# First DFT of an AFNO block on one Trainium2 core: normalization factors folded into the DFT matrix, other queues for the last rows, another order of the lower weight parts

## Chip, cores and metric

The kernel runs on one core of a Trainium2 chip. The metric is the time of one execution on the device in microseconds (us). The engines are named as in the profile: PE (TensorE, matmul), DVE (VectorE), ACT (ScalarE), POOL (GpSimd) and SP (SyncE, which here only issues DMAs).

## What is computed

An adaLN block on 4096 rows of 640 values: layer norm of x with a scale and a shift from `c`, a spectral mixer (a 2-D real FFT over a 1 x 4096 grid, a two-layer block MLP per frequency, an inverse FFT), then layer norm and a SwiGLU feed-forward. The change touches only the start: layer norm, FFT and the weights of the two layers.

```python
    x = A_x
    mod = (_silu(c) @ w_mod).reshape(c.shape[0], 6, 1, -1)
    sa, ca, ga, sb, cb, gb = ...
    h = _layernorm(x, axis=-1) * (1 + ca) + sa
    x = x + ga * _A_ref(h, A_w1, A_b1, A_w2, A_b2)
    h = _layernorm(x, axis=-1) * (1 + cb) + sb
    x = x + gb * _B_ref(h, B_w_gate, B_w_up, B_w_down)

def _A_ref(x, w1, b1, w2, b2):
    Xf = rfft2(x, axes=(1, 2))              # H = 1, so one FFT of length 4096 per channel
    z = Xf.reshape(B, H, Wf, NB, BS)        # NB = 4 blocks of BS = 160 channels
    hr = zr @ w1[0] - zi @ w1[1] + b1[0];  hi = zi @ w1[0] + zr @ w1[1] + b1[1]
    hr, hi = relu(hr), relu(hi)
    or_, oi_ = (the same with w2, b2), then soft-shrink by 0.01
    return irfft2(or_ + 1j * oi_)
```

## The kernel before

**The FFT in two stages.** A row index is written as n = 32 n1 + n2. Stage A is a DFT over n1 (128 points): the partitions of a tile hold n1, so one matmul with the constant matrix `fa` (128 x 128) transforms one n2. Stage B is a DFT over n2 (32 points, matrix `tb`) for a chunk of frequencies; there are eight chunks (`NCH`). Behind stage B comes the first layer (`stage_l1`, with `w1a`, `w1b`, `w1c`), then the second (`stage_l2`, with `w2a`, `w2b`, `w2c` and the bias `b2t`), the soft-shrink and the first inverse stage.

**Stage A.** x is read as eight tiles `xa` of four n2 each: 128 partitions x 4 rows x 640. For each tile `ln_stats` (L401) takes mean and variance of each row on DVE, two statistics of 320 values per row, and forms `rs` (1/sqrt of the variance, by a power) and `nm` (minus mean times `rs`) on POOL. `ln_apply` (L411) normalizes every row over its 640 values, some rows on ACT and some on DVE. `dft_a` (L432) makes five matmuls of 512 columns: rows 0 to 3 with the first 128 channels of each of the four blocks, and a fifth with the remaining 32 channels of all rows and blocks. In fp32 each matmul is two passes on PE. `evac_a` (L442) copies the results back into `xa`. The loop runs `ln_stats(t + 2)`, `ln_apply(t + 1)`, `dft_a(t)`, `evac_a(t)`, `moves(t)`.

**From stage A to stage B.** The frequencies have to be brought together over all n2. Most go through four scratch tensors `s1` in DRAM (`write_s1`, then `load_g`). For chunk 0 the rows of the last two tiles go straight from SBUF to SBUF: `move_g` copies four pieces of each of tiles 6 and 7 into `g0`, two of the four on POOL's DMA queue and two on SP's.

**What sets the order.** Everything in this part is in program order on each engine (`manual_schedule`), so an instruction waits for its data and everything behind it on its engine waits too. The order on SP's queue is the order of the calls in `moves(t)`: a write that waits for ACT holds up the loads behind it.

**Weights in two parts.** The first and second layers multiply rounded values (fp32r) in a high and a low part. `weights_high` writes the high part (POOL for the first six of the twelve `w1` jobs, ACT for the other six), `weights_low` the lower part on DVE (value times sign, minus the high part, L286). Jobs 0 to 5 are for the first half of the outputs, 6 to 11 for the second; of six jobs three are 512 wide and three 128. The lower parts of `w2` are made by DVE (jobs `w2a`, `w2b`, `w2c`) and POOL (`weights_rest`).

**The scale 1 + ca and the second bias.** `first_scale` accumulates five products of `w_mod` and silu(c) on DVE into `acc0`, `remainders` copies its 32-channel ends into `wx0`, `columns` sums over the partitions on PE, and `ca1` is the result. `c` is loaded behind tile 6 of x. The second bias `b2` is loaded into one partition of `b2s`, spread to all partitions by three matmuls with ones (L481) and copied to `b2t` by ACT (L487). `idle(n)` is n matmuls whose result nobody reads.

**Stage B of chunk 0.** `stage_b` (L600) makes the DFT over n2 for blocks 0 and 4 (the remainders) and 1; `evac_b` writes `z` in a high part by ACT (L607) and a lower by DVE (L608), `evac_r` the same for the remainders `rz` (L630 on ACT, L640 on DVE).

Of the kernel before, what the change touches and what calls it, by code (L numbers as in the profile page):

```python
# [173 lines left out]
def body(tc, x, w1, b1, w2, b2, wg, wu, wd, c, wm, k_fa, k_tb, k_tx, k_bm, k_bx, k_ga, k_ge, k_id, out, dbg=None):  # L174
# [4 lines left out]
    def f32(ap):  # L179
        return ap.bitcast(F32)  # L180
# [21 lines left out]
    with ExitStack() as top:  # L202
# [35 lines left out]
        with ExitStack() as af:  # L238
# [50 lines left out]
            af.enter_context(tc.manual_schedule())  # L289
            nc.sync.dma_start(fa, k_fa)  # L290
# [45 lines left out]
            stx = ExitStack()  # L336
            xp = stx.enter_context(tc.tile_pool(name="xp", bufs=1, side="right"))
            rp = af.enter_context(tc.tile_pool(name="rp", bufs=1))
            b2t = rp.tile([P, 2, NB, BS], F32, name="b2t")
            with tc.tile_pool(name="sp", bufs=1) as sp:  # L340
                xas = []
                xts = {t: xp.tile([P, 4, D], F32, name=f"xa{t}") for t in (1, 2, 3, 0, 4, 5, 6, 7)}

                def load_x(t):
                    xa = xts[t]
                    if t < 3:
                        for i in range(4):
                            nc.sync.dma_start(xa[:, i, :], xv[:, 4 * t + i, :])
                    else:
                        nc.sync.dma_start(xa, xv[:, 4 * t:4 * t + 4, :])  # L350
                    xas.append(xa)


                def write_s1(t, f):
                    nc.sync.dma_start(s1[f][4 * t:4 * t + 4].rearrange("n r d -> r n d"),
                                      xas[t][(slice(0, 64, 4), slice(64, P, 4), slice(2, P, 4), slice(1, P, 2))[f]])

                for t in range(6):
                    load_x(t)
                wm1 = sp.tile([P, 5, D], F32, name="wm1")  # L360
                stats = {}
                pas = {}
                raws = {}


                def moves(t):
                    if t < 6:
                        write_s1(t, 0)
                    if t < 4:
                        write_s1(t, 1)  # L370
                    if t == 0:
                        load_x(6)
                        nc.sync.dma_start(c5, c)
                    elif t == 1:
                        load_x(7)
                        raws[1] = load_weights(sp, w1, "1")
                    elif t == 2:
# [2161 lines left out]
```

## Time and profile before

| quantity | value |
|---|---|
| time, median of 3 runs | 1412.85 us (1411.89 to 1417.92) |
| profiled execution: time | 1411.32 us |
| profiled execution: span from the first to the last instruction | 1409.5 us |
| granted PE clock | 1.0 |
| busy over the span: PE, DVE, ACT, POOL | 98%, 76%, 54%, 43% |
| busy from 18 to 40 us (22 us): PE, DVE, ACT, POOL | 20.09, 21.60, 19.92, 10.55 us |
| busy from 50 to 56 us (6 us): PE, DVE, ACT, POOL | 4.58, 5.18, 4.81, 2.42 us |
| first matmul of stage A | 7.98 us |
| last matmul of stage A ends | 49.3 us |
| first matmul of stage B | 55.84 us |

Times in a timeline are microseconds from the start of the span. A row of the timeline gives start, length, engine, line, operation, what is written and read, a count where neighbours are merged, and in brackets how long the engine stood idle ahead of it and what ended that. "L286" is line 286 of the kernel. Lengths of neighbours can overlap, since an engine begins one instruction while the one before it drains.

### The profile page before, as it was taken

To read this page: it belongs to the slowest core of one execution; us is meant where nothing else is said; L and a number is where in the kernel's file an instruction comes from. 1 tells how busy PE (TensorE), PEld (TensorE's weight loads), DVE (VectorE), ACT (ScalarE), POOL (GpSimd) and SP (SyncE) were. 2 spreads that over 40 slices of the span, in tenths; PEclk is the share of its full clock that TensorE was granted. 3 is DMA by queue.
4 is the path that set the end of the run, shared out by engine and by line. 5 is a ranking of instruction groups with operands and counts; after the bars stand their busy time and mean duration, and the time that the engine had idled before them with its cause. 6 is when DMAs were issued, how large, how long until landed. Compare 5 with 4: busy or idle time off the path is not lost. (4 is left out here: it accounts for less than half of the span.)

```text
span 1409.5 us, 23754 instructions
## 1 busy us (share of the span) xinstructions
PE 1382.5 (98%) x8410; PEld 1310.7 (93%) x8410; DVE 1067.8 (76%) x1861; ACT 765.0 (54%) x1542; POOL 604.6 (43%) x683
## 2 busy tenths in 40 slices
PE   6899999999999999999999999999999999999998
PEld 2599999967999889899999999999999999999998
DVE  8889888889888888649787668678678757375644
ACT  6879999755555554436454345546164624262341
POOL 5700200157766594326445534447153624042241
PEclk9999999999999999999999999999999999999999
DMA  9876466675998897898877998696998668956634
GB/s 371 310 244 211 157 196 193 203 232 170 327 353 308 308 335 263 293 368 308 308 225 281 375 330 288 236 326 230 375 330 309 217 218 282 350 194 217 199 115 149
DMA packets 171016, 377.34 MB, mean 268 GB/s; under 512 B 22193, under 2 KB 81649, under 8 KB 168882
## 3 DMA queue, kind: packets, MB, share of 16 engines
q1 hardware_dynamic: 161794, 359.28, 73.6%
q0 software_dynamic: 6800, 13.93, 3.1%
q10 hardware_dynamic: 2304, 2.62, 0.5%
q8 instruction: 66, 1.08, 0.3%
q14 instruction: 52, 0.43, 0.1%
HBM read 269.48 MB, written 96.80 MB: 260 GB/s over the span
## 5 line engine op out<-in xcount | busy, mean ns | idle before, releaser
L1442 DVE TENSOR_TENSOR wb<-r,wb 128x768 fp32r<-128x768 f32 (+3 forms) x170 | 170.4, 1013 | 13.5 <-ACT wb L1435 13.3
L2050 PE MATMUL pw<-h,wt 128*128 128x384 f32 x412 | 139.3, 338 | 0.6 <-ACT s_y L2069 0.6
L2052 PE MATMUL pw<-h,wt 128*128 128x384 f32 x412 | 138.3, 336 | 0.0
L2051 PE MATMUL pw<-h,wt 128*128 128x384 f32 x412 | 138.1, 335 | 0.0
L1435 ACT ACTIVATE wb<-r 128x768 fp32r<-128x768 f32 (+3 forms) x168 | 104.5, 639 | 56.3 <-PE pw L2063 41.7
L2351 PE MATMUL pc<-wq,L 128*128 128x320 f32 x846 | 132.7, 309 | 0.9 <-DMA wq<-wqd 0.9
L2110 POOL TENSOR_TENSOR sg<-s_x,sg 128x384 f32<-128x384 f32 x24 | 30.0, 1250 | 234.5 <-DVE s_x L2076 234.5
L2351 PEld LDWEIGHTS pc<-wq,L 128*128 128x128 f32 x846 | 126.3, 188 | 1.1 <-DVE x L2308 1.1
L2130 DVE TENSOR_TENSOR L<-sg,L 128x384 fp32r<-128x384 f32 x144 | 101.0, 725 | 27.7 <-ACT L L2126 27.2
L2069 ACT ACTIVATE s_x<-pw 128x384 f32<-128x384 f32 x52 | 25.6, 492 | 164.2 <-PE pw L2052 162.3
L2050 PE MATMUL pw<-h,wb 128*128 128x384 f32 x312 | 105.0, 336 | 0.0
L2051 PE MATMUL pw<-h,wb 128*128 128x384 f32 x312 | 104.4, 335 | 0.0
L2052 PE MATMUL pw<-h,wb 128*128 128x384 f32 x312 | 104.4, 335 | 0.0
L2121 POOL TENSOR_TENSOR sg<-sg,sg 128x384 f32<-128x384 f32 x72 | 91.9, 1276 | 23.4 <-DVE L L2130 20.0
L1973 PE MATMUL pg<-ht,wb 128*128 128x512 f32 x260 | 101.8, 392 | 0.0
L2351 PE MATMUL pe<-wq,L 128*128 128x320 f32 x648 | 101.7, 309 | 0.0
L1974 PE MATMUL pg<-ht,wb 128*128 128x512 f32 x260 | 101.3, 390 | 0.0
L1975 PE MATMUL pg<-ht,wb 128*128 128x512 f32 x260 | 101.2, 389 | 0.0
L2267 PE MATMUL pd<-wq,a 128*128 128x320 f32 x632 | 96.8, 310 | 0.0
L2351 PEld LDWEIGHTS pe<-wq,L 128*128 128x128 f32 x648 | 96.6, 188 | 0.0
L2267 PEld LDWEIGHTS pd<-wq,a 128*128 128x128 f32 x632 | 93.5, 188 | 0.5
L772 POOL DMA_DIRECT2D s<-co x28 | 15.7, 559 | 175.9 <-ACT co L771 175.9
(317 smaller groups left out, 3914.1 us busy)
## 6 DMA issues: line engine op xcount, KB each, us to landing
wq<-wqd SPq DMA_DIRECT2D x83, 640.0 KB, 6.1
wt<-td SPq DMA_DIRECT2D x103, 512.0 KB, 5.4
hs<-ho SPq DMA_DIRECT2D x52, 512.0 KB, 5.2
h<-hs SPq DMA_DIRECT2D x32, 768.0 KB, 7.9
td<-wt SPq DMA_DIRECT2D x25, 512.0 KB, 6.3
r<-in_B_w_gate_dram SPq DMA_DIRECT2D x24, 384.0 KB, 4.4
r<-in_B_w_up_dram SPq DMA_DIRECT2D x24, 384.0 KB, 4.3
xx<-tt SPq DMA_DIRECT2D x56, 160.0 KB, 3.3
```

Of the source, the lines that this page charges most:

```text
L1435: def high(ks, e=slice(0, c), copy=lambda o, i: act.activation(o, i, AF.Copy)):
L1442: dve.tensor_tensor(wbs[t, n][:, 1, ks, e], raw[t, n][:, ks, e], f32(wbs[t, n][:, 0, ks, e]), op=OP.subtract)
L1973: mm(b, wh, hh, start=(kk == 0), stop=False)
L1974: mm(b, wh, hl, start=False, stop=False)
L1975: mm(b, wl, hh, start=False, stop=(kk == 4))
L2050: mm(b, w(0, kp), a[:, kp, 0], start=start and kp == 0, stop=False, skip_group_check=not start)
L2051: mm(b, w(0, kp), a[:, kp, 1], start=False, stop=False, skip_group_check=not start)
L2052: mm(b, w(1, kp), a[:, kp, 0], start=False, stop=kp == 1, skip_group_check=not start)
L2121: pool.tensor_tensor(o, x, y, op=op)
L2130: dve.tensor_tensor(o[:, 1], raws[j], f32(o[:, 0]), op=OP.subtract)
L2267: mm(b[:, :320], l, m, start=start and i == 0, stop=stop and i == len(s) - 1)
L2351: mm(o[:, :320], ls[q][:, x, k], w[:, q, y], start=start and q == 0 and n == 0, stop=q == 1 and n == 2, skip_group_check=not start)
```

## The change

**Normalization in the DFT matrix.** For tiles 1 to 6 the rows are no longer normalized over 512 of their 640 channels. `scaled` multiplies the DFT matrix `fa` by `rs` (a factor per partition, that is per n1) for each row, into `wts` (rows 0 to 2 on ACT, row 3 on POOL; for tile 1 all on ACT). The matmul of a row uses its own scaled matrix. The mean's part is a sixth product per tile: `fa` with the four columns `nm`; `bias_a` copies its result to `bts`, and the evacuation of rows 0 to 3 adds it as a bias per partition. The remaining 4 x 32 channels of a row are still normalized in place (`rest`: rows 0 and 1 on ACT, 2 and 3 on DVE). Tiles 0 and 7 keep whole normalized rows (`ln_row`: ACT for tile 0, DVE for tile 7).

**Order of stage A.** Statistics are formed in groups of two rows (tiles 2 to 7), one tile ahead of the DFT instead of two, and the evacuation of a tile stands behind the preparation of the next. All evacuations are on ACT but one, row 3 of tile 7.

**Queues.** Of the eight `move_g` copies only one, row 0 of tile 7, stays on POOL's queue; seven are on SP's. `c` is loaded first on ACT's queue, and silu(c) comes at once. `b2` is loaded into all partitions by one DMA behind the loads of chunk 1, instead of one partition, matmuls and copies. The first half of `w2` is loaded behind the writes of tile 5 and 1.

**Other edits.** Fourteen idle matmuls stand at the start and six, not four, ahead of stage B. Of the lower parts of `w1`, job 0 stands ahead of the last evacuation, 1 to 5 ahead of `ca1`, 6 ahead of the first `z`, and 7 to 11 behind the first `rz`. `stage_b`, `evac_b` and `evac_r` are moved up in the text and `rz` goes to another pool.

```diff
+            nc.scalar.dma_start(c5, c)
             nc.sync.dma_start(fa, k_fa)
...
+                act.activation(sc, c5, AF.Silu)
+                idle(14)
...
                     if t < 6:
                         write_s1(t, 0)
+                    else:
+                        for i in range(4):
+                            move_g(0, t, i, pool if t == 7 and i == 0 else nc.sync)
...
-                        nc.sync.dma_start(c5, c)
...
-                        nc.sync.dma_start(b2s[0:1], b2.rearrange("r b o -> (r b o)").unsqueeze(0))
                     elif t == 4:
                         load_g(0, (0, 1))
-                        raws[2] = load_weights(rp, w2, "2", (0,))
                     elif t == 5:
                         for f in (2, 3):
                             write_s1(1, f)
+                        raws[2] = load_weights(rp, w2, "2", (0,))
                     elif t == 6:
-                        for i in range(4):
-                            move_g(0, t, i, (pool, nc.sync)[i // 2])
                         load_g(0, (2,))
-                    elif t == 7:
-                        for i in range(4):
-                            move_g(0, t, i, (pool, nc.sync)[i // 2])
...
+                def ln_stats(t, rows=range(4)):
+                    n = 1 if t < 2 else 2
+                    for i in rows[::n]:
                         mv, rs = layer_stats(lp, xas[t][:, i:i + n, :], n, f"a{t}_{i}")
...
+                def ln_row(t, i):
...
+                def scaled(t, *rows):
...
+                    for i in rows:
+                        if t > 1 and i == 3:
+                            pool.tensor_scalar(wts[t][:, i, :], fa, stats[t, i][1], None, op0=OP.mult)
+                        else:
+                            act.activation(wts[t][:, i, :], fa, AF.Copy, scale=stats[t, i][1])
+
+                def rest(t, *rows):
+                    for i in rows:
                         mean, rs, nm = stats[t, i]
+                        v = xas[t][:, i, :].rearrange("p (b e) -> p b e", b=NB)[:, :, 128:160]
+                        if i < 2:
+                            act.activation(v, v, AF.Identity, bias=nm, scale=rs)
                         else:
+                            dve.tensor_scalar(v, v, mean, rs, op0=OP.subtract, op1=OP.mult)
...
                 def dft_a(t):
                     xnr = xas[t].rearrange("p a (b e) -> p a b e", b=NB)
+                    plain = t in (0, 7)
+                    for i in (4, 0, 1, 2, 3) if t == 7 else (0, 1, 2, 3, 4) if t == 0 else (0, 1, 2, 3, 5, 4):
+                        pa = pas[t, i] = bank_a(f"pa{t}_{i}")
+                        if i == 5:
+                            mm(pa[:, 0:4], fa, nms[t], start=True, stop=True)
+                        elif i == 4:
+                            mm(pa, fa, xnr[:, :, :, 128:160], start=True, stop=True)
+                        else:
+                            mm(pa, fa if plain else wts[t][:, i, :], xnr[:, i, :, 0:128], start=True, stop=True)
+
+                def bias_a(t):
+                    bts[t] = sp.tile([P, 4], F32, tag="bt", bufs=3, name=f"bt{t}")
+                    act.activation(bts[t], pas[t, 5][:, 0:4], AF.Copy)
...
+                        elif t in bts:
+                            act.activation(xa[:, i, 0:512], pas[t, i], AF.Identity, bias=bts[t][:, i:i + 1])
...
+                for t in range(2, 7):
+                    ln_stats(t + 1, A)
+                    rest(t, 2, 3)
+                    ln_stats(t + 1, B)
+                    if t < 6:
+                        scaled(t + 1, 3)
+                    scaled(t, 0, 1)
+                    bias_a(t - 1)
+                    rest(t, 0, 1)
+                    if t == 2:
+                        evac_a(1, 0, 1)
+                    scaled(t, 2)
+                    evac_a(t - 1, *((2, 3) if t == 2 else (0, 1, 2, 3)))
+                    evac_a(t - 1, 4)
                     dft_a(t)
+                    moves(t - 1)
+                prep1 = prep_weights(raws[1], w1a, w1b, w1c, True)
+                for job in prep1[:6]:
+                    weights_high(*job, pool)
+                for i in range(4):
+                    ln_row(7, i)
+                first_scale(0, 3)
+                bias_a(6)
+                evac_a(6, 0, 1, 2, 3, 4)
+                dft_a(7)
+                moves(6)
+                first_scale(3, 5)
+                remainders(acc0, wx0)
+                weights_low(*prep1[0])
+                evac_a(7, 0, 1, 2, 3, 4)
+                moves(7)
 
                 pm1 = columns(acc0, wx0)
...
+                idle(6)
                 for job in prep1[6:]:
                     weights_high(*job)
...
+                for job in prep1[1:6]:
                     weights_low(*job)
+                dve.tensor_scalar(ca1, pm1[:, 0:5], 1.0, None, op0=OP.add)
...
+                load_tb(1)
+                nc.sync.dma_start(b2t.rearrange("p r b o -> p (r b o)"),
+                                  b2.rearrange("r b o -> (r b o)").unsqueeze(0).to_broadcast([P, 2 * NB * BS]))
...
+                for n in (1, 0):
+                    weights_high(*prep2[n])
+                weights_low(*prep1[6])
+                evac_b(0, 0)
+                evac_r(0, 0)
+                for job in prep1[7:]:
+                    weights_low(*job)
```

The order of instructions, as the built programs have it. First ACT, one tile in the middle of stage A. Before: the normalization of tile 5's first rows (`xa_120`), then the five evacuations of tile 4 (`xa_119`), then two rows of tile 6.

```order
L418 ACTIVATE xa_120<-xa_120,nm_0_384,rs_a_0_381 128x640 x3
L450 ACTIVATE xa_119<-pa_0_437 128x512
L450 ACTIVATE xa_119<-pa_1_439 128x512
L450 ACTIVATE xa_119<-pa_2_441 128x512
L450 ACTIVATE xa_119<-pa_3_443 128x512
L448 ACTIVATE xa_119<-pa_4_445 128x4x128
L418 ACTIVATE xa_121<-xa_121,nm_0_430,rs_a_0_427 128x640 x2
```

Now: two scaled matrices of tile 4 (`wt_395`), the bias of tile 3 (`bt_457`), remainders of two rows of tile 4 (`xa_120`), the third matrix, then the evacuations of tile 3 (`xa_118`).

```order
L491 ACTIVATE wt_395<-fa,rs_a_0_374 128x128 x2
L531 ACTIVATE bt_457<-pa_5_417 128x4
L498 ACTIVATE xa_120<-xa_120,nm_377,rs_a_0_374 128x4x32 x2
L491 ACTIVATE wt_395<-fa,rs_a_2_390 128x128
L541 ACTIVATE xa_118<-pa_0_409,bt_457 128x512
L541 ACTIVATE xa_118<-pa_1_411,bt_457 128x512
L541 ACTIVATE xa_118<-pa_2_413,bt_457 128x512
L541 ACTIVATE xa_118<-pa_3_415,bt_457 128x512
L537 ACTIVATE xa_118<-pa_4_419 128x4x128
```

The row products of 640 are gone, and six short instructions per tile stand in their place.

Then POOL, from the last square roots of tile 7 to the copy into `g0`. Before:

```order
L197 TENSOR_SCALAR rs_a_0_473<-mv_a_0_460 128x4
L198 TENSOR_TENSOR rs_a_0_473<-rs_a_0_473,mhalf 128x4
L406 TENSOR_TENSOR nm_0_476<-mv_a_0_460,rs_a_0_473 128x4
L407 TENSOR_TENSOR nm_0_476<-nm_0_476,mone 128x4
L281 TENSOR_SCALAR w1a<-rm_320 128x4x128
L281 TENSOR_SCALAR w1b<-rm_320 128x4x128
L281 TENSOR_SCALAR w1c<-rr_321,sgn 128x4x128
L281 TENSOR_SCALAR w1a<-rm_320 128x4x32
L281 TENSOR_SCALAR w1b<-rm_320 128x4x32
L281 TENSOR_SCALAR w1c<-rr_321,sgn 128x4x32
L316 DMA g_453<-xa_121 4x4x640 x2
L316 DMA g_453<-xa_122 4x4x640 x2
```

Now, from the scaled matrix of tile 6 (`wt_514`) on:

```order
L489 TENSOR_SCALAR wt_514<-fa,rs_a_2_509 128x128
L197 TENSOR_SCALAR rs_a_0_552<-mv_a_0_545 128x2
L198 TENSOR_TENSOR rs_a_0_552<-rs_a_0_552,mhalf 128x2
L197 TENSOR_SCALAR rs_a_2_565<-mv_a_2_558 128x2
L198 TENSOR_TENSOR rs_a_2_565<-rs_a_2_565,mhalf 128x2
L281 TENSOR_SCALAR w1a<-rm_362 128x4x128
L281 TENSOR_SCALAR w1b<-rm_362 128x4x128
L281 TENSOR_SCALAR w1c<-rr_363,sgn 128x4x128
L281 TENSOR_SCALAR w1a<-rm_362 128x4x32
L281 TENSOR_SCALAR w1b<-rm_362 128x4x32
L281 TENSOR_SCALAR w1c<-rr_363,sgn 128x4x32
L317 DMA g_541<-xa_123 4x4x640
```

Statistics are worked on in two halves, the means of tile 7 are not formed, and one copy stands behind the six products where four stood.

Last DVE, around the first `z` of stage B. Before, all lower parts of `w1` stand ahead of it:

```order
L286 SCALAR_TENSOR_TENSOR w1a<-rm_320,w1a 128x4x128
L286 SCALAR_TENSOR_TENSOR w1b<-rm_320,w1b 128x4x128
L286 SCALAR_TENSOR_TENSOR w1c<-rr_321,w1c 128x4x128
L286 SCALAR_TENSOR_TENSOR w1a<-rm_320,w1a 128x4x32
L286 SCALAR_TENSOR_TENSOR w1b<-rm_320,w1b 128x4x32
L286 SCALAR_TENSOR_TENSOR w1c<-rr_321,w1c 128x4x32
L608 SCALAR_TENSOR_TENSOR z_0_663<-pb_0_646,ca_68,z_0_663 128x2x256
L640 SCALAR_TENSOR_TENSOR rz_666<-pb_4_651,ca_68,rz_666 32x256 x2
L608 SCALAR_TENSOR_TENSOR z_1_671<-pb_1_656,ca_68,z_1_671 128x2x256
```

Now:

```order
L286 SCALAR_TENSOR_TENSOR w1a<-rm_362,w1a 128x4x128
L359 SCALAR_TENSOR_TENSOR z_0_734<-pb_0_716,ca_68,z_0_734 128x2x256
L391 SCALAR_TENSOR_TENSOR rz_737<-pb_4_721,ca_68,rz_737 32x256 x2
L286 SCALAR_TENSOR_TENSOR w1b<-rm_362,w1b 128x4x128
L286 SCALAR_TENSOR_TENSOR w1c<-rr_363,w1c 128x4x128
L286 SCALAR_TENSOR_TENSOR w1a<-rm_362,w1a 128x4x32
L286 SCALAR_TENSOR_TENSOR w1b<-rm_362,w1b 128x4x32
L286 SCALAR_TENSOR_TENSOR w1c<-rr_363,w1c 128x4x32
L359 SCALAR_TENSOR_TENSOR z_1_751<-pb_1_726,ca_68,z_1_751 128x2x256
```

Five of the six lower parts of the second half moved from ahead of the first `z` to behind the first `rz`.

427 lines of the change are left out of this document (208 added, 219 removed).

## Prediction

> **What bounds the kernel now.** First the table of stretches, busy time of each engine in pieces of the span: one row of the loop over x, one from behind it.
>
> ```profile
> core 0: us, PE busy (x) PEld busy (x) DVE busy (x) ACT busy (x) POOL busy (x), PEclk, DMA share, GB/s
> 18.00:40.00 22.00, 20.09 (x46) 8.06 (x45) 21.60 (x69) 19.92 (x34) 10.55 (x21) 1.00 1.01 410
> 80.00:120.00 40.00, 40.00 (x318) 40.00 (x317) 34.05 (x68) 35.37 (x74) 1.13 (x2) 1.00 0.60 190
> ```
>
> From 80 us on PE is busy all the time, so what the change gains or loses in the first DFT reaches the end only as far as it moves the point from which PE no longer stops. The waits of PE between 56 and 72 us say where that point lies:
>
> ```profile
> PE pb L600 <- DMA g<-xa: 1.4, 1, 1.4
> ...
> PE pc L711 <- DVE w2c L286: 0.5, 1, 0.5
> ```
>
> Two things count: when the last rows of x land in `g0` (L600, stage B), and when DVE has finished the lower part of `w2c`. The timeline of DVE, with PE's start of stage B:
>
> ```profile
> 54.53 0.69 DVE L286 SCALAR_TENSOR_TENSOR w1b<-rm,w1b 128x512 fp32r<-128x512 f32 x1
> ...
> 56.14 0.28 DVE L286 SCALAR_TENSOR_TENSOR w1c<-rr,w1c 128x128 fp32r<-128x128 f32 x1
> 57.73 0.75 DVE L608 SCALAR_TENSOR_TENSOR z<-pb,ca,z 128x512 fp32r<-128x512 f32 x1 [1.31 <-ACT z L607]
> 58.87 0.97 DVE L640 SCALAR_TENSOR_TENSOR rz<-pb,ca,rz 32x256 fp32r<-32x256 f32 x2 [0.40 <-ACT rz L630]
> ...
> 60.85 0.98 DVE L640 SCALAR_TENSOR_TENSOR rz<-pb,ca,rz 32x256 fp32r<-32x256 f32 x2 [0.23 <-ACT rz L630]
> ...
> 65.98 1.69 DVE L286 SCALAR_TENSOR_TENSOR w2b<-rm,w2b 128x640 fp32r<-128x640 f32 x1
> ...
> 69.16 0.89 DVE L286 SCALAR_TENSOR_TENSOR w2c<-rr,sgn,w2c 128x640 fp32r<-128x640 f32 x1
> ...
> 55.84 2.92 PE L600 MATMUL pb<-tb,g 128*128 128x128 f32 x24 [1.43 <-DMA g<-xa]
> ```
>
> From the first `z` at 57.73 to the end of `w2c` at 70.05 DVE stands still only 0.40 + 0.23 us: this chain of 12.32 us, hung on stage B's start, sets PE's last stop, at 70.2. The five lower parts from 54.53 to 56.42 (1.89 us) are free, since DVE then waits 1.31 us for stage B.
>
> What sets 55.84 is POOL, which copies four pieces of x into `g0` behind its six `w1` products. Its timeline, and the row of those copies among the DMAs (microseconds to landing last):
>
> ```profile
> 39.24 1.25 POOL L198 TENSOR_TENSOR rs_a<-rs_a,mhalf 128x4 f32<-128x4 f32 x1
> ...
> 41.28 1.75 POOL L281 TENSOR_SCALAR w1a<-rm 128x512 fp32r<-128x512 f32 x1
> ...
> 47.56 1.01 POOL L281 TENSOR_SCALAR w1c<-rr,sgn 128x128 fp32r<-128x128 f32 x1
> 48.53 1.40 POOL L316 DMA_DIRECT2D g<-xa  x2
> 50.23 1.13 POOL L316 DMA_DIRECT2D g<-xa  x2 [0.30 <-ACT xa L448]
> ...
> g<-xa POOLq DMA_DIRECT2D x4, 40.0 KB, 5.0
> ```
>
> Products from 41.28 to 48.57 (7.29 us), four copies, the last issued in the second half of 50.23 to 51.36, that is near 50.8, and 5.0 us to landing: 55.8.
>
> **The loop over x, engine by engine.** Three rows of the timeline (statistics and aggregates of one tile on DVE, the last four tiles on PE), then groups of the first 72 us by shape (busy, mean ns):
>
> ```profile
> 18.16 3.24 DVE L193 BATCH_NORM_STATS2 st_a<-xa 128x6 f32<-128x320 f32 x8
> 21.33 0.41 DVE L195 BATCH_NORM_AGGREGATE mv_a<-st_a 128x2 f32<-128x12 f32 x4
> ...
> 31.56 17.74 PE L439 MATMUL pa<-xa,fa 128*128 128x512 f32 x40 [1.81 <-ACT xa L418]
> ...
> 35.04 3.24 DVE L193 BATCH_NORM_STATS2 st_a<-xa 128x6 f32<-128x320 f32 x8
> ...
> L416 DVE TENSOR_SCALAR xa<-xa,mv_a,rs_a 128x640 f32<-128x640 f32 x13 | 7.4, 608 | 0.9 <-POOL rs_a L198 0.9
> L418 ACT ACTIVATE xa<-xa,nm,rs_a 128x640 f32<-128x640 f32 x19 | 16.9, 928 | 5.3 <-POOL nm L407 5.3
> L450 ACT ACTIVATE xa<-pa 128x512 f32<-128x512 f32 x28 | 14.6, 604 | 2.0 <-PE pa L439 1.9
> L607 ACT ACTIVATE z<-pb,ca 128x512 fp32r<-128x512 f32 x4 | 2.8, 689 | 1.9 <-PE pb L600 1.8
> L283 ACT ACTIVATE w1a<-rm 128x128 fp32r<-128x128 f32 x1 | 0.3, 298 | 0.0
> L198 POOL TENSOR_TENSOR rs_a<-rs_a,mhalf 128x4 f32<-128x4 f32 x6 | 7.1, 1177 | 0.5
> L198 POOL TENSOR_TENSOR rs_a<-rs_a,mhalf 128x1 f32<-128x1 f32 x8 | 4.5, 569 | 0.7
> L281 POOL TENSOR_SCALAR w1c<-rr,sgn 128x128 fp32r<-128x128 f32 x1 | 1.0, 1012 | 0.0
> L281 POOL TENSOR_SCALAR w1a<-rm 128x128 fp32r<-128x128 f32 x1 | 0.5, 523 | 0.0
> L430 DVE SCALAR_TENSOR_TENSOR acc<-wm,sc,acc 128x640 f32<-128x640 f32 x4 | 3.8, 952 | 0.1
> L446 DVE COPY xa<-pa 128x512 f32<-128x512 f32 x4 | 2.6, 683 | 0.5 <-PE pa L439 0.5
> ```
>
> *DVE* was full in this loop (21.60 of 22.00). A tile's eight statistics take 3.24 us, four aggregates 0.41; both stay. One to four row products of 608 ns go; two remainders of a fifth of the elements come, whose price lies between that fifth, 0.12, and the whole 0.61; I take 0.2 each, near the lower end. With the aggregates in two groups instead of one (up to 0.2 more) that is 4.05 to 4.25 us per tile. Now the statistics of tiles 3 and 7 begin 16.88 us apart, 4.22 per tile. DVE gains next to nothing: the statistics fill it, not the products.
>
> *ACT.* Out go two or three row products of 928 ns per tile. In come three scaled matrices (above 298, the same width without a factor per partition, and below 689, four times as wide with one; 390 taken), a copy of four columns (below 298; 200 taken), two remainders (298 to 928; 450 taken), and a bias in four evacuations: 689, the same width with one such operand, for 604. With the fifth evacuation as now that is 5.6 us, less some 0.09 for each of eleven neighbours that overlap: 4.6 to 4.7 us per tile. The second table load leaves the stream.
>
> *PE.* A tile's ten passes take 17.74 / 4 = 4.4 us, and a small product of four columns joins them (below one product more, 0.9; 0.1 taken): 4.5.
>
> *POOL.* Per half tile the power is 0.77 (on the line from 569 at one column to 1177 at four), with three short ones and gaps 1.8 us; two halves and one scaled matrix of 0.52 to 1.01 us make 4.1 to 4.6 us. With one power of 1177 for a whole tile it was about 2.5.
>
> So four engines end between 4.05 and 4.7 us per tile, and the loop doesn't get shorter. Ahead of tile 3 DVE has the same statistics as now, so its start stays near 18; the last aggregates then come at 18.0 + 5 x 4.25 = 39.2. POOL, by then some 0.4 behind, needs 1.2 for the last square root and starts the products at 40.8, against 41.28.
>
> **The sum.** Products 40.8 + 7.29 = 48.1; one copy there, landing 5.0 later, and 0.3 to PE as now: stage B at **53.4**, 2.4 us earlier. The three copies on SyncE come late too: DVE normalizes its last two rows until 42.1, forms `acc0` (five of 952 ns) and `wx0` (0.3) until 47.2, one lower part until 47.8, then copies row 3 (683 ns) until 48.5. How long 40 KB take on that queue no row shows; the bounds are
>
> ```profile
> fa<-in_k_fa_dram SPq DMA_DIRECT2D x1, 64.0 KB, 1.9
> ...
> s<-xa SPq DMA_DIRECT2D x14, 160.0 KB, 6.7
> ```
>
> and so a landing between 51.0 (with 0.6 of issue) and 55.8; with 4 us, between the two since other transfers run, 53.1: beside POOL's. Then the new order gives back: five lower parts, 1.89 us, stand between `rz` and the second `z`, in the chain that has only 0.23 us of slack there: 1.7 us. POOL's `w2` products, beside which `w2b`'s lower part took 1.69 against 0.89 for `w2c`, are then about 1 us further on; that is worth 0 to 0.8, and I take 0.5. **Net gain 2.4 - 1.7 + 0.5 = 1.2 us.**
>
> Costed at nothing, with what hides it: the idle passes at the start (PE waits for the first row); the sums of the second bias and their copies, which go (PE and ACT wait for 55.84 there; without that cover they would be worth 2.4 us); four moves of tile 6 on SyncE, which waits for ACT then; and `w2`'s first half, now loaded behind three writes: its reader on ACT comes just ahead of stage B's first `z`, so that a late load would hold up `z`, and DVE behind it, by as much. The bias, now 640 KB behind `tb` of chunk 1:
>
> ```profile
> 65.69 0.57 SPq L298 DMA_DIRECT2D tb<-in_k_tb_dram  x1
> ...
> 73.38 0.89 DVE L713 TENSOR_TENSOR tt<-pc,b2t 128x320 f32<-128x320 f32 x2
> ```
>
> Issued 0.6 behind `tb`, 2.4 earlier than now, and landing within 6.7 us it is there at 70.6; DVE wants it at 72.2. If it is late, `h` and `u` behind it on DVE wait, and PE for them.
>
> The profiled execution took 1411.32 us (span 1409.5), 1.5 less than the median of the runs shown, 1412.85. Less 1.2 these are 1410.1 and 1411.6; I take **1411.0**.
>
> **Rivals.**
>
> *DVE is the bound.* If SyncE's small copies land in 2 us and POOL's products run in half their time, DVE runs through: copy until 48.5, five lower parts and `ca1` 2.5, a sixth 0.6, then the chain, 12.3 + 1.7: 65.6 against 70.05, 4.5 us less: 1407.5. For it: the order of the lower parts would then cost nothing. Against it: the 7.29 us of the six products are in the trace, and they start behind the same statistics. 0.22.
>
> *POOL holds the loop back, and the new order costs.* Two rows show POOL's spread at one shape and operation; the first ran beside DVE's lower parts:
>
> ```profile
> L528 POOL TENSOR_TENSOR w2a<-rm,w2a 128x640 fp32r<-128x640 f32 x1 | 3.1, 3114 | 3.4 <-ACT w2a L283 3.4
> L528 POOL TENSOR_TENSOR w2b<-rm,w2b 128x640 fp32r<-128x640 f32 x1 | 1.5, 1542 | 0.1
> ```
>
> If a tile takes POOL 5.1 us instead of 4.6, five tiles put its products 2.5 us later, at 43.3, stage B at 55.9, and the lower parts then cost their 1.7 us: 1413.3. The sign turns where the products start at about 42.0. For it: POOL's work per tile nearly doubles, in short instructions beside a full DVE. Against it: beside the same statistics the power takes its 1177 ns now. 0.17. [...]
>
> **Chances.** Forecast 0.54 (1409.5 to 1412.5), DVE bound 0.22, POOL 0.17, the rest 0.07: a late `w2`, bias or load of x, or a gain beyond DVE's. The range, 1406.0 to 1415.0, takes in the first three and the spread of the runs shown. 0.5% is about 7 us, what a measurement of this kernel can tell from no change; no case reaches it but the tails: faster 0.04, same 0.94, slower 0.02.
>
> **What would show it.** POOL's first `w1` product at 40.8 (42.0 or later: the rival); stage B at 53.4, released by a copy into `g0`; five lower parts between `rz` and the second `z`, `w2c` done near 68.9, and PE without a stop from there. The forecast is wrong if stage B comes before 50, or if DVE waits for the bias, the statistics for x, or ACT for `w2`.

## Result and the profile after

| | kernel before | changed kernel |
|---|---|---|
| time, median | 1412.37 us (4 runs, 1410.84 to 1417.92) | 1420.30 us (4 runs, 1419.37 to 1422.65) |
| profiled execution: time, span | 1411.32, 1409.5 us | 1419.37, 1417.6 us |
| granted PE clock over the span | 1.000 | 0.994 |

The ratio is 1.0058, 95% interval 1.0038 to 1.0078: slower by about 8 us, where 1.2 us less had been forecast. Timed again beside the kernel before (e6 below), it was 1420.42 against 1413.65 us, ratio 1.0040 (1.0024 to 1.0056).

The loop over x itself went as planned. These are the stretches of the changed kernel, the same columns as before, with the two in which stage B starts, then the kernel before around its stage B:

```profile
core 0: us, PE busy (x) PEld busy (x) DVE busy (x) ACT busy (x) POOL busy (x), PEclk, DMA share, GB/s
18.00:40.00 22.00, 22.00 (x58) 10.08 (x58) 21.64 (x73) 21.73 (x53) 16.98 (x45) 1.00 1.01 418
50.00:60.00 10.00, 5.53 (x26) 5.56 (x27) 2.50 (x7) 2.47 (x6) 8.88 (x5) 0.68 0.92 324
60.00:70.00 10.00, 8.60 (x64) 7.83 (x63) 9.78 (x18) 8.51 (x19) 3.40 (x5) 0.98 0.91 300
80.00:120.00 40.00, 40.00 (x317) 40.00 (x316) 33.90 (x68) 34.99 (x72) 1.12 (x2) 1.00 0.54 183
```

```profile
50.00:56.00 6.00, 4.58 (x25) 3.41 (x26) 5.18 (x13) 4.81 (x11) 2.42 (x3) 1.00 0.78 203
56.00:70.00 14.00, 11.32 (x89) 10.47 (x88) 11.83 (x20) 11.63 (x24) 12.10 (x9) 1.00 0.95 360
```

From 18 to 40 us PE, DVE and ACT are all full. From 50 to 60 us DVE and ACT work a quarter of the time and PE about half of it, and the column PEclk reads 0.68, where the kernel before has 1.00. The timeline says what PE and SyncE did there, and POOL's first product and copy:

```profile
40.29 1.51 POOL L281 TENSOR_SCALAR w1a<-rm 128x512 fp32r<-128x512 f32 x1
47.01 1.05 PE L328 MATMUL pmc<-ones,acc 128*128 128x1 f32 x8 [0.24 <-DVE acc L509]
48.23 0.79 POOL L317 DMA_DIRECT2D g<-xa  x1
48.14 1.82 SPq L317 DMA_DIRECT2D g<-xa  x3
48.14 1.58 PE L335 MATMUL pz<-ones 128*128 128x128 f32 x12
54.47 5.46 PE L351 MATMUL pb<-tb,g 128*128 128x128 f32 x24 [4.74 <-DMA rr<-in_A_w_dram]
57.28 0.75 DVE L359 SCALAR_TENSOR_TENSOR z<-pb,ca,z 128x512 fp32r<-128x512 f32 x1 [6.27 <-ACT z L358]
60.24 0.69 DVE L286 SCALAR_TENSOR_TENSOR w1b<-rm,w1b 128x512 fp32r<-128x512 f32 x1
60.84 2.05 DVE L286 SCALAR_TENSOR_TENSOR w1c<-rr,w1c 128x512 fp32r<-128x512 f32 x1
70.10 0.88 DVE L286 SCALAR_TENSOR_TENSOR w2c<-rr,sgn,w2c 128x640 fp32r<-128x640 f32 x1
```

Before, PE did this ahead of stage B:

```profile
49.99 1.05 PE L327 MATMUL pmc<-ones,acc 128*128 128x1 f32 x8 [0.69 <-ACT xa L448]
51.13 2.40 PE L481 MATMUL pb<-b2s,ones 128*128 128x512 f32 x6
53.36 1.05 PE L334 MATMUL pz<-ones 128*128 128x128 f32 x8
```

Stage B starts at 54.47 instead of 55.84, but its 24 passes take 5.46 us instead of 2.92, after PE stood still for 4.74 us instead of 1.43. (The releaser named is a load of `w2`, which stage B does not read.) Of the eight copies into `g0`, the trace has a landing for the one on POOL's queue alone:

```profile
g<-xa POOLq DMA_DIRECT2D x1, 40.0 KB, 5.1
```

It was issued at 48.23 and so had landed at 53.3, 1.1 us before PE started. What was still to land then was on SyncE's queue.

The lower part of `w2c` starts at 70.10 instead of 69.16. Fine stretches of the same kernel give the clock around this place and around two later ones:

```profile
53.50:54.25 0.75, 0.00 (x0) 0.00 (x0) 0.00 (x0) 0.00 (x0) 0.75 (x2) 0.58 0.88 290
54.25:55.00 0.75, 0.53 (x2) 0.56 (x3) 0.00 (x0) 0.00 (x0) 0.75 (x1) 0.50 1.01 406
59.50:60.25 0.75, 0.75 (x6) 0.75 (x5) 0.70 (x3) 0.28 (x1) 0.67 (x2) 0.50 0.85 294
60.25:61.00 0.75, 0.75 (x7) 0.75 (x7) 0.75 (x2) 0.72 (x2) 0.75 (x1) 0.87 1.27 352
326.50:327.00 0.50, 0.50 (x3) 0.50 (x4) 0.50 (x2) 0.00 (x0) 0.00 (x0) 0.69 1.10 442
329.50:330.00 0.50, 0.50 (x3) 0.41 (x2) 0.30 (x1) 0.00 (x0) 0.00 (x0) 0.50 1.07 383
514.67:515.33 0.66, 0.66 (x4) 0.66 (x4) 0.49 (x1) 0.06 (x1) 0.00 (x0) 0.50 0.76 131
516.67:517.33 0.66, 0.66 (x4) 0.66 (x3) 0.66 (x2) 0.05 (x1) 0.00 (x0) 0.50 1.09 377
```

Summed over all stretches, the clock is at half for 6.8 us from 53.6 us on, for 3.4 us from 326.7 and for 3.4 us from 514.4, and for no time in the profile of before. (A last stretch, at the end of the span, lies behind the last matmul and is left out here and below.) PE's waits, the longest of after, then the same two products in before (`py` is a product of the last inverse stage, `gt` its matrix, loaded on POOL's queue, and `chl` the lower part of its input, made by DVE):

```profile
PE pb L351 <- DMA rr<-in_A_w_dram: 4.7, 1, 4.7
PE py L1749 <- DMA gt<-in_k_ga_dram: 4.1, 1, 4.1
PE py L1749 <- DVE chl L1739: 2.0, 1, 2.0
```

```profile
PE py L1688 <- DMA gt<-in_k_ga_dram: 1.5, 1, 1.5
...
PE py L1688 <- DVE chl L1678: 0.8, 1, 0.8
```

So each half-clock stretch of after begins in a wait or just behind one: at 53.62 us in the wait that ends with stage B at 54.47, at 326.69 behind the wait for `chl` that ends at 326.39, and at 514.42 behind the one for `gt` that ends at 513.93. Where the 8.1 us of span come from is seen by the start of the same instruction in both traces (after less before): `pl` at 72 us +0.9, `pt` at 306 us +1.2, the first `pd` behind `py` at 352 us +2.7, the first `pw` behind the other `py`, at 610 us, +6.8, the last matmul +6.6, and the last store of the output 1.5 more.

Where `chl` is late, near 324 us, DVE and POOL meet. First the changed kernel, then the kernel before, DVE and POOL:

```profile
324.18 2.15 DVE L1739 TENSOR_TENSOR chl<-cr,chh 128x640 fp32r<-128x640 f32 x1
322.10 3.55 POOL L1604 TENSOR_TENSOR wdr<-wdr,gbb 128x640 f32<-128x640 f32 x2
```

```profile
324.37 0.81 DVE L1678 TENSOR_TENSOR chl<-cr,chh 128x640 fp32r<-128x640 f32 x1
320.30 3.73 POOL L1543 TENSOR_TENSOR wdr<-wdr,gbb 128x640 f32<-128x640 f32 x2
```

In before POOL's two products end at 324.03, just ahead of `chl`; after, they run until 325.65 beside it, and the same subtraction takes 2.15 us instead of 0.81. `gt` near 510 us is a DMA on POOL's queue; it was issued at 508.00 instead of 504.40 and landed in 5.8 us instead of 4.1.

### The profile page after: what moved, and what is told of

Its sections match the earlier page's. It is cut to its first block, busy times and chain, and to the rows that moved or that the text cites. A ratio compares the mean times of both kernels' runs of the same rounds, so it can differ in the third digit from the quotient of the medians.

```text
span 1417.6 us, 23876 instructions
## 1 busy us (share of the span) xinstructions
PE 1391.4 (98%) x8448; PEld 1322.0 (93%) x8448; DVE 1064.3 (75%) x1861; ACT 766.2 (54%) x1563; POOL 605.9 (43%) x696
```

## Experiments

Theory "clock": PE's clock falls to half behind a long wait, ahead of stage B first of all, because the sums of the second bias no longer keep PE at work. Rival "order": the new order of the lower parts and of the transfers makes the chain late, and the clock only goes with it. Each kernel was timed beside the kernel before (medians 1413.35 for e1 to e4, 1413.65 for e5 to e8, 1413.47 for e9 to e12, 1414.04 for e13 to e16, from 24 to 35 runs each). Effects are given as differences of medians. The ratio isn't that of the medians and often gives less: against e6, e1 is 4.2 us faster by the ratios and 6.1 by the medians, e4 3.0 and 4.1, e10 4.4 and 6.2. A profile is one execution; those of e2, e4, e8 and e16 are the slowest of their sets. `px`, ten small products near 142 us, serves as a mark of how late the chain is there.

| run | median us | ratio to before, 95% | half clock in its profile: from us, for us |
|---|---|---|---|
| e1 after, 22 idle | 1414.32 | 0.9993 to 1.0027 | none |
| e2 before, bias by DMA | 1413.45 | 0.9991 to 1.0023 | 55 3.4, 79 3.4, 516 3.4 |
| e3 before, 14 idle | 1412.34 | 0.9981 to 1.0015 | 509 3.4 |
| e4 after, lower parts first | 1416.29 | 1.0004 to 1.0034 | 52 6.8, 325 3.4, 510 6.8 |
| e5 after, e1 + e4 | 1413.48 | 0.9986 to 1.0015 | 57 3.4, 326 3.4, 746 3.4 |
| e6 after again | 1420.42 | 1.0024 to 1.0056 | 54 3.4, 327 3.4, 512 6.8 |
| e7 before, idle at two py | 1421.54 | 1.0029 to 1.0065 | 513 6.8 |
| e8 e5, idle at two py | 1418.69 | 1.0016 to 1.0039 | 76 3.4, 513 6.8 |
| e9 before, gt early | 1411.03 | 0.9973 to 0.9995 | none |
| e10 after, gt early | 1414.25 | 0.9998 to 1.0020 | 56 6.8, 329 3.4 |
| e11 e5, bias early | 1414.17 | 0.9986 to 1.0009 | 325 3.4 |
| e12 e11, gt early, idle at first py | 1408.30 | 0.9956 to 0.9981 | none |
| e13 after, gt early, idle at first py | 1412.32 | 0.9980 to 0.9998 | 54 6.8 |
| e14 e13, 22 idle | 1410.53 | 0.9967 to 0.9987 | none |
| e15 before, gt early, idle at first py | 1410.76 | 0.9962 to 0.9986 | 71 3.4 |
| e16 e13, lower parts first | 1410.67 | 0.9962 to 0.9982 | 54 6.8 |

**e1: more idle matmuls ahead of stage B.**

```diff
-                idle(6)
+                idle(22)
```

> The changed kernel with 22 idle matmuls ahead of stage B instead of 6, so that PE works until about 53.9 us, nearly until stage B's rows are there. Theory 'clock': PE stood still from 49.72 to 54.47 us, and the granted clock was 0.50 from 53.8 to 60.4 us; the 24 passes of stage B took 5.46 us instead of 2.92. With PE kept at work the clock stays 1.0, the 24 passes take about 2.9 us, w2c is done near 69 us, and the time is 1409 to 1413 us. Theory 'order': the new order of the lower parts and of SyncE's transfers makes stage B's chain late and the clock only goes with it: w2c at 70.5 us or later and 1417 us or more.

Clock 1.0 in the whole profile, and 6.1 us less than the changed kernel in e6. The time came out 1.3 us above the range, and `w2c` at 69.54 us, between the two theories: the clock is a large part, and something else is left.

**e2: the bias alone, in the kernel before** (no sums, no copies, one DMA behind the loads of chunk 1).

```diff
-                    mm(pbs2[n][:, :w], ones, b2s[:, 512 * n:512 * n + w], start=True, stop=True)
-                act.activation(b2v[:, 512 * n:512 * n + w], pbs2[n][:, :w], AF.Copy)
+            nc.sync.dma_start(b2t.rearrange("p r b o -> p (r b o)"), b2....to_broadcast([P, 2 * NB * BS]))
```

> The kernel before with one part of the change: the second bias comes by one DMA to all partitions behind the loads of chunk 1, and the three sums with ones and the three copies are gone. PE then has nothing to do from about 52.2 us to stage B at 55.84. Theory 'clock': the granted clock falls to 0.50 in stage B, its first 24 passes take over 4 us instead of 2.92, and the time is 1414 to 1421 us. Theory 'order': the sums lay beside a wait, and the time stays within 1 us of before.

The mechanism came as expected, the price did not. PE's wait ahead of stage B grew from 1.4 to 2.6 us, the clock is at half from 55.1 to 58.5 us in its profile, and no execution reached a mean of 1.0, but stage B began at 54.94 in that execution, and the median stayed. Its waits show a new one, the bias itself:

```profile
PE pc L703 <- DVE tt L705: 2.5, 1, 2.5
```

**e3: a later stage B in before.** `idle(4)` became `idle(14)`.

> The kernel before with 14 idle matmuls ahead of stage B instead of 4: PE stays at work, but stage B begins about 1.2 us later, near 57.0 us, at clock 1.0. Theory 'a late start is paid again': the same wait for chl at 324 us grows from 0.8 to about 2.0 us with the clock at 0.50 for some 3.4 us behind it, and again at 503 us for gt, so the time is 1416 to 1421 us. Theory 'one for one': 1412.4 + 1.2, within 0.5 of 1413.6 us.

This run could not decide: stage B began at 56.15, only 0.3 later than in the profile of before, so that the delay wasn't there to be paid.

**e4: the lower parts in the old order.**

```diff
-                for job in prep1[1:6]:
+                for job in prep1[1:]:
                     weights_low(*job)
...
-                weights_low(*prep1[6])
...
-                for job in prep1[7:]:
-                    weights_low(*job)
```

> The changed kernel with the lower parts of w1 in the order of before (all of 1 to 11 ahead of ca1, none between z and rz): DVE has 6.27 us free ahead of the first z, so they cost nothing there. Theory 'clock': stage B still starts near 54.4 at clock 0.50, the chain from z to w2c is 1 to 2 us shorter (w2c near 69.5), and the time falls by 1 to 2 us, to 1418 to 1419, or further only as far as the later waits shrink. Theory 'order': this is the main loss and the time is 1410 to 1413 us.

4.1 us less than e6, more than "clock" allowed and less than "order" wanted. Stage B began at 55.58, still at half clock, and yet `w2c` started at 68.17. Neither theory holds alone; e13 to e16 price both.

**e5: both edits of the start.**

> The changed kernel with both edits: 22 idle matmuls ahead of stage B, and all lower parts of w1 but the first ahead of ca1. Theory 'two separate losses at the start, clock and order': stage B at 54.5 to 55.6 us at clock 1.0, the lower part of w2c starts 12.6 us behind stage B less what the half clock cost there (11 to 12.5 us, so 66 to 68 us), and px (142.55 us in the changed kernel, 141.45 before) comes at 139 to 140 us; the time is 1409 to 1413 us, with what the waits near 325 and 510 us add on top in some executions. Rival 'one of the two hides the other': px within 0.4 us of the better of the two edits alone (140.58 us).

The time is right, px (141.86 us) is not: the start gained and lost it again. DVE's timeline of e5, and of e8, where the rows of stage B had landed earlier (53.73 us):

```profile
75.50 0.89 DVE L787 TENSOR_TENSOR tt<-pc,b2t 128x320 f32<-128x320 f32 x2 [3.24 <-DMA s<-xa]
```

```profile
74.47 0.89 DVE L787 TENSOR_TENSOR tt<-pc,b2t 128x320 f32<-128x320 f32 x2 [5.34 <-DMA s<-xa]
```

`tt` is the first reader of the second bias. However early the chain is, it goes on when the bias has landed, at 74 to 75.5 us.

**e6: the changed kernel again.**

> The changed kernel itself, timed again beside the kernel before, for the spread of its executions: by 'the clock in stage B falls in every execution' no execution has a mean granted clock above 0.998, and its median lies 3 to 8 us above before; by 'one unlucky set of runs' some executions reach clock 0.999 or 1.0 and 1411 us.

Six executions, all between 1418.13 and 1421.22 us with a mean clock of 0.994 to 0.996. It is no unlucky set. The kernel before spreads from 1410.12 to 1418.57 us beside it.

**e7 and e8: idle matmuls in the later waits.**

```diff
+                    for _ in range({4: 6, 8: 12}.get(r, 0) if hf == 0 else 0):
+                        mm(py[hf][0][:, :128], ones, ones, start=True, stop=True)
```

> The kernel before, with idle matmuls on PE ahead of two products much later: 6 ahead of the first py (near 324 us, where PE waits 0.8 to 2.0 us for chl) and 12 ahead of the fifth (near 507 us, where it waits 1.5 to 4.2 us for gt). They fill waits; where a wait is short they add up to 1.4 us each. Theory 'the spread of before, 1410.2 to 1419.1 us, is the clock falling behind these two waits in some executions': the slow tail goes, no execution below clock 0.998, median 1410 to 1413 us. Theory 'the spread lies elsewhere': the same share of executions above 1415 us as before (about a third).

> The changed kernel with all three kinds of edit: 22 idle matmuls ahead of stage B, the lower parts ahead of ca1, and the idle matmuls ahead of the first and the fifth py. If the losses are the clock at three places and the order, the sum is a kernel that beats both: px near 139.5 us, clock 0.999 or 1.0 in nearly all executions, 1408 to 1411 us, and 1 to 3 us below the kernel before in the median. If the start doesn't reach the end, it equals the kernel before with the same fillers.

Both missed, by a mistake of mine: row 8 is not the row whose `gt` is late; that is row 10, the ninth in order. The 12 matmuls stood near 420 us, where nothing waits, and cost their time, while the wait at row 10 was 3.4 and 3.7 us with the clock at half for 6.8 us behind it. What they show all the same: at the first `py` the 6 matmuls left a wait of 0.6 us for `chl`, and no half clock.

**e9 and e10: gt for row 10 issued earlier**, in before and in after.

```diff
                 def g_in():
+                    if r in gtr:
+                        return
...
+                    if (r, hf) == (9, 1):
+                        row_load(10)[2].f()
```

> The kernel before, with one transfer issued earlier on POOL's queue: gt for row 10 (the 128 KB that PE waits for near 507 us) right behind the products of row 9 instead of 16 instructions later, behind a square root that waits for DVE. Theory 'the wait for gt and the half clock behind it are a large part of the spread of before (1410.1 to 1419.1 us)': the wait of 1.5 us or more at that py goes, and the median falls by 2 to 4 us, to 1409.5 to 1411.5. Theory 'PE would wait there for something else': another wait of 1.5 us or more stands at the same product and the median stays within 1 us.

> The changed kernel with the same transfer (gt for row 10) issued earlier. In its two profiles PE waits 4.1 and 4.4 us there and the granted clock is 0.50 for 3.4 and 6.8 us behind it. Theory 'a late start is paid a second time there': the median falls by 5 to 7 us, to 1413.5 to 1415.5, and what is left is the start (about 1 us), the clock behind chl near 326 us (1.7) and chance. Theory 'the start alone carries the loss': it falls by no more than the kernel before does from the same edit.

Both as the first theory had them: 2.4 us less than before, and 6.2 us less than the changed kernel in e6. The wait for `gt` is gone from both, and of 6.8 us between the two kernels 3.2 are left.

**e11: the bias earlier on SyncE's queue.** Its DMA stands behind the first four writes (issued at 55.55 us, not 64.4).

> The changed kernel with 22 idle matmuls, the lower parts ahead of ca1, and the DMA of the second bias moved up on SyncE's queue from behind the loads of chunk 1 to behind the first four of the writes (near 52.5 us instead of 64.4). With the first two edits alone DVE stood idle 3.24 us ahead of the first tt and PE 1.1 us at it, and 5.34 and 2.6 us in a profile where stage B began at 53.73. Theory 'the bias takes the place of the waits removed': the idle time ahead of tt falls below 1 us, px comes at 139 to 140.5 us instead of 141.86, and the median is 1 to 2 us below the kernel before. Theory 'PE's stop there has another cause': px stays at 141.5 or later.

px comes at 140.31 us instead of 141.86: the bias had been the stop. DVE still waited 1.88 us at `tt`, and the median did not follow. The later waits were there (1.7 us for `gt`, 1.9 for `chl`, and 2.2 for `wq` near 744 us, which was 2.6 in e5, with a half clock behind it, and 1.4 or less elsewhere); that they took the gain is likely, not shown.

**e12: all of it.**

> All of it: the changed kernel with 22 idle matmuls, lower parts ahead of ca1, the bias moved up, gt for row 10 issued earlier, and 6 idle matmuls (1.4 us) ahead of the first py near 324 us, where PE waits 2.0 us for chl. If these are the places where the change lost, px comes at 139 to 140.5 us, most executions have clock 0.999 or 1.0, and the median is 1407 to 1410 us, 3 us or more below the kernel before. If the gain at the start is lost again on the way, it stays at 1411 us or more.

1408.30 us, ratio 0.9956 to 0.9981: it beats both kernels. Its waits ahead of stage B and at `chl` are short:

```profile
PE pb L351 <- DMA rr<-in_A_w_dram: 1.4, 1, 1.4
...
PE py L1750 <- DVE chl L1738: 0.6, 1, 0.6
```

Much of that gain is open to the kernel before too (e15), by two edits that have nothing to do with this change; what e12 has beyond e15 is not clear of the noise.

**e13 to e16: the start alone.** With `gt` early and 6 idle matmuls at the first `py`, the wait for `gt` is gone, 0.6 us of wait for `chl` are left, and no half clock follows, in the changed kernel (e13), with 22 idle matmuls (e14), in the kernel before (e15), and with the lower parts first (e16).

> The changed kernel with the two later waits out of the way: gt for row 10 issued earlier, and 6 idle matmuls ahead of the first py near 324 us. Theory 'the half clock behind the first py is in the loss': 1.0 to 2.0 us below the same kernel without the idle matmuls (1414.25), so 1412 to 1413.5 us. Theory 'what is left is the start alone': within 0.7 us of 1414.25.

> The changed kernel with the two later waits out of the way and 22 idle matmuls ahead of stage B. The difference to e13 is what the half clock in stage B costs alone: 1 to 2 us by the profiles (from stage B's start to the lower part of w2c 15.6 us at half clock and 14.35 without), so 1410.5 to 1412 us; no difference if the chain on DVE hides it.

> The kernel before with the two later waits out of the way, the measure for the other three. In its profile PE waits 0.8 us for chl, where the 6 idle matmuls take 1.4, so they may cost 0.6 us, or gain where the clock fell there: 1410 to 1412 us, and 1 to 3 us below e13 if the start of the changed kernel is the slower one, equal to it if all of the loss lay in the two later waits.

> The changed kernel with the two later waits out of the way and all lower parts of w1 but the first ahead of ca1. The difference to e13 is what their new order costs alone: by the prediction 1.7 us; by the profiles at half clock 15.6 less 12.6, that is 3.0 us from stage B to w2c, of which px keeps 2; so 1409.5 to 1411.5 us. If stage B at half clock hides the order, no difference.

All four medians lie in their ranges. PE and DVE of e13, then of e14:

```profile
55.05 5.46 PE L351 MATMUL pb<-tb,g 128*128 128x128 f32 x24 [4.82 <-DMA rr<-in_A_w_dram]
70.67 0.89 DVE L286 SCALAR_TENSOR_TENSOR w2c<-rr,sgn,w2c 128x640 fp32r<-128x640 f32 x1
```

```profile
48.20 5.16 PE L335 MATMUL pz<-ones 128*128 128x128 f32 x44
54.91 2.92 PE L351 MATMUL pb<-tb,g 128*128 128x128 f32 x24 [1.55 <-DMA g<-xa]
69.09 0.88 DVE L286 SCALAR_TENSOR_TENSOR w2c<-rr,sgn,w2c 128x640 fp32r<-128x640 f32 x1
```

Same start, 1.6 us at `w2c`: that is the half clock, and the medians say 1.8 us (1412.32 less 1410.53). The order costs 1.65 (1412.32 less 1410.67). The changed start as a whole is 1.56 us slower than that of before (1412.32 less 1410.76); with the clock kept (e14) the two are equal within the noise (1410.53 and 1410.76).

The order took more than 1.65 from DVE's chain, as the profile of e16 shows beside that of e13 above:

```profile
68.30 0.88 DVE L286 SCALAR_TENSOR_TENSOR w2c<-rr,sgn,w2c 128x640 fp32r<-128x640 f32 x1
75.04 0.89 DVE L787 TENSOR_TENSOR tt<-pc,b2t 128x320 f32<-128x320 f32 x2 [2.55 <-DMA s<-xa]
```

`w2c` came 2.4 us earlier, and then DVE waited 2.55 us at `tt`, where the bias is read.

**The sum.** By medians, the 6.8 us between the kernels are 1.6 at the start, 1.6 at the first `py` (3.2 less 1.6) and 3.6 at `gt` (6.8 less 3.2). By the middles of the ratios they are 2.1, 1.4 and 2.1 of 5.7 us (1.0040; 1.0009 less 0.9984; 0.9989 less 0.9974). By the scatter of the single executions each term is known to 1 to 2 us: those of the start and of `gt` are clear of zero, that of the first `py` is not. That the idle matmuls there help the changed kernel is clear (e13 against e10); that the wait costs it more than it costs the kernel before is likely, not shown.

## Why the prediction was wrong

- **The loop over x: right.** The first product of `w1` was to start at 40.8 and started at 40.29. Three engines are full (22.00, 21.64 and 21.73 of 22 us), POOL was costed too high (16.98), and a tile takes DVE 4.1 us instead of 4.2: next to nothing gained in length.
- **Stage B at 53.4, 2.4 us earlier: half right.** The last copies were issued by 49.96 and stage B began 4.5 us later, at 54.47. Four profiles of the changed kernel that are alike up to there (after, e6, e10, e13) give 54.47, 54.62, 56.20 and 55.05, four of before (before, e7, e9, e15) 55.84, 56.17, 57.66 and 55.97: 1.3 us earlier in the mean, not 2.4. The mis-sized term is the copies on SyncE's queue, taken to land at 53.1, "beside POOL's". POOL's copy did land there (53.3 in after), but PE started 0.9 to 1.4 us behind it in all four profiles. That it waited for SyncE's copies, whose landing the trace doesn't give, is the reading that is left, not a measurement.
- **The order of the lower parts gives back 1.7, and POOL's relief is worth 0.5: right in sum, by luck in part.** The median says 1.65 for the order (e16 against e13), after the bias had taken back part of 2.4 us. Between the first `rz` and the second `z` the five parts took 3.2 us in after and 3.5 in e14, not 1.9, since one of them met POOL's product for `w2c` (in after 2.05 us instead of about 0.7). In return `w2a`, `w2b` and the first `h` took 2.4 us in e14 where 4.8 were spent before, beside POOL. From the first `z` to `w2c` that makes 12.3 us at full clock (e14) against 11.4 before: a loss of 0.9 where 1.7 - 0.5 = 1.2 was forecast, from two terms that were each too small.
- **The step that failed first: the sums of the second bias, costed at nothing, since "PE and ACT wait for 55.84 there".** The text priced them at 2.4 us were their cover gone, and the cover stayed; but the sums also kept PE at work. They are about half of it: of the 3.3 us by which PE's wait grew, 1.7 are work that went. The other 1.6 are a move that the prediction didn't look at: PE's sums for `ca` (`columns`) began at 47.01 instead of 49.99, 3.0 us earlier, and stage B only 1.4. So PE stood still for 4.7 us, the clock was at half for 6.8 us, and stage B's passes took 5.46 us instead of 2.92. The half clock alone cost 1.8 us (e14 against e13). The bias's sums alone, taken out of the kernel before (e2), left a wait of 2.6 us and no loss that can be told from noise. The two views to see it in were there: what PE does ahead of stage B, and PEclk, which the prediction read as 1.00 and didn't ask when it would stay so. In after it was 0.50 for 6.8 us from 53.62 on, after 3.9 us of the wait of 4.74, and near 326 us a wait of 1.98 us was enough for 3.4 us of it (see the last section).
- **The step that failed most: one for one.** "From 80 us on PE is busy all the time, so what the change gains or loses in the first DFT reaches the end only as far as it moves the point from which PE no longer stops." PE does stop again, for `chl` and for `gt`. The view of waits that the prediction quoted was cut to 56 to 72 us; over the whole span it lists both, 0.8 and 1.5 us. With these two out of the way the rule fits: e13 is 1.5 us behind e15 at `w2c` in their profiles (70.67 and 69.16) and 1.56 at the end by the medians. Each of the two waits had two lengths in the profiles (0.6 to 0.8 or about 2.0; 1.4 to 1.7 or 3.2 to 4.4 us), and half clock followed both longer ones in after (3.4 us each), e4 and e6 (3.4 us at `chl`, 6.8 at `gt`), though not the 2.0 us for `chl` in e1. That cost 5.2 of the 6.8 us by medians (3.5 of 5.7 by ratios). For `chl` the subtraction ran beside POOL's product in after and e6, and just behind it in before and e9; but e3 has it beside and a wait of 0.6. What picks the lengths is open. It isn't lateness alone: e4 was ahead of before at px (140.58 against 141.45 us) and had both long, e1 was 0.5 us late there and had the short one for `gt`.
- **The bias: named, mis-sized.** It was to be there at 70.6; it let DVE go on at 74 to 75.5. In the changed kernel the late chain hid that (`tt` at 74.32 without a wait); with the chain earlier it became the next stop (e4, e5, e8, e16), as e11 showed by moving it.
- **A late `w2`** did not happen: ACT began its first half at 49.46, long before stage B.
- **The rivals:** "POOL holds the loop back" is refuted by 40.29; "DVE is the bound" never got its chance, as DVE stood idle 6.27 us ahead of the first `z`. A forecast with the right terms would have been 1.3 for stage B, less 0.9 for the chain, less 1.8 for the clock, slower by about 1.5 us at the start (measured 1.56), and a note that two waits of PE further on can multiply it.

## What to carry to other kernels

Work that lies beside a wait isn't free to remove when it is what keeps PE at work: add up PE's idle time ahead of a stage as it will be, not as it is, and if it nears the 2.0 us that were followed by half clock at `chl` in after, put idle matmuls there (ahead of stage B they were worth 1.8 us, e14 against e13). A shift of one microsecond early in a kernel was not carried to the end one for one here (+0.9 us at 72 us, +6.6 at the last matmul): read the list of waits for all later places where PE stops for 0.5 to 2 us, and ask what each becomes when its neighbours move; a transfer issued earlier there can be worth more than the stage being tuned (`gt` for row 10: 6.2 us, e10 against e6; the changed start: 1.56, e13 against e15). When two causes hide each other, first take the later amplifiers out of both kernels, then measure each cause alone.

## What the runs showed of the hardware

- Half-clock stretches were 3.4 or 6.8 us long in every profile that has one (the table of the experiments), but for those at the end of the span. In after the three were 6.83, 3.41 and 3.41 us long and began at 53.62, 326.69 and 514.42 us, and the clock granted in them was 0.50.
- Ahead of stage B, PE's waits of 4.74 us in after, 5.9 in e4, 5.8 in e10, and 4.8 in e13 and e16 each came with 6.8 us of half clock. Of shorter ones there, 2.6 us in e2 came with 3.4 us of it, and 2.9 in e9, 2.0 in e1, 1.9 in e11, 1.6 in e14 and 1.4 in before with none.
- Waits of about 2 us for `chl` went both ways: 1.98 us in after, 2.0 in e4 and e10 and 1.9 in e11 were followed by 3.4 us of half clock, 2.0 in e1 and e2 were not. For `gt`, 4.1 us in after, 4.2 in e4 and 3.7 in e2 were followed by it, and 1.4 in e1, 1.5 in before and 1.7 in e11 were not. In e15 waits of 1.08 and 0.54 us close together, which ended at 69.28 and 70.19 us, were followed by 3.4 us of half clock from 71.5 on; before had the same two (1.07 and 0.53 us), and its clock stayed at 1.0. So one and the same wait cost the clock in one profile and not in another; what decides is not shown.
- The subtraction for `chl`, 128 x 640 on DVE, took 0.81 us in before, where POOL's products of the same size had just ended, and 2.15 in after, where one of them ran beside it.
- Behind the same copies of 40 KB stage B began up to 1.8 us apart from profile to profile (54.47 to 56.20 us in the changed kernel, 55.84 to 57.66 in before). The executions of the kernel before spread over 10 us (1408.69 to 1419.10 in the 31 timed beside e13 to e16); nine of the ten fastest have a mean clock of 0.999 or 1.000, and three of the ten slowest.
